# Query blocks turned through DRAM instead of TensorE, and six weight portions converted later, in an attention block followed by two MLPs

## The chip, the cores and the metric

One core of one Trainium2 chip. The metric is the device time of one execution, in microseconds (us): the median of the kernel before is 1572.41 us over three runs (1571.00 to 1572.81).

## The reference

Eight batches with eight heads of 576 positions and 64 features go through an efficient attention; its output is laid out as 4608 tokens of 512 features, which pass a first MLP with a hard gate and a second one with a sigmoid gate. All is float32.

```
q_s = softmax(q over features); k_s = softmax(k over positions)
x   = q_s @ (k_s.T @ v)              # per batch and head; then 4608 x 512
h   = x @ w_in;  g = h * clip(h + 3, 0, 6) / 6;  x = g @ w_out    # 512 -> 2048 -> 512
h   = x @ w2_in; g = h * sigmoid(h);             out = g @ w2_out
```

## The kernel before

Every product is made of matmuls on numbers split in two: a rounded upper part (fp32r) and the rest, three matmuls for one product (upper by upper, upper by lower, lower by upper). Twelve matmuls of 128x512 make one half step of an MLP.

**Blocks, units, stages.** The tokens are nine blocks of 512 (`NB`). The attention of a block is four units (`NP`), each a pair of heads, so there are 36 units, u = 0 to 35. The kernel has three stages:

- `first_block` does units 0 to 7 whole, a part of 8, the first MLP's weights and the first MLP on block 0.
- `middle` does the rest of the attention (q and x of units 8 to 35, k and v to unit 31) between the matmuls of the first MLP on blocks 1 to 4 (steps of `mm1`, L606, gate, `mm2`, L675). It also makes from both MLPs' weights the sums that the third stage needs, and stores them to DRAM (`ws`). Each of 16 portions of the second MLP's weights is loaded raw (`load_w`, L149), put together in float32 out of two words (`Conv`, L167: two scales on ScalarE, `shift`, `round`, `sign` on VectorE), split and stored (`Split`, L268), summed on GpSimd (`sums_in_place`, L244), split and stored again. The 16 portions of the first MLP's weights are already on the chip (`Resident`, L307).
- `second_mlp` runs six passes, each over a pair of blocks, with Strassen-like sums (seven products for eight), then the last block of the second MLP alone. `PASSES` (L112) orders them as (MLP, first block): (1,1), (0,5), (0,7), (1,3), (1,5), (1,7), 0 being the first MLP and 1 the second. A pass has 56 inner steps and 56 outer steps of six matmuls each; its weights come from `ws` through a ring of six buffers of 512 KB, each refilled as soon as it is used (`fetch`, L1268). Everything in a pass is put in order by a time in steps (`when`, L1254).

**The order in the middle** is written out: every piece of work is a job with an engine, and `MIDDLE` (L24) is the list of job numbers (two digits to base 64, the jobs numbered as `add` is called). Each engine runs its own jobs in that order; the keys (`begin`, `at`) do not decide there. SP issues all transfers, in order, so a transfer whose input is late holds back all that follow it.

**A unit's query path in the middle.** `q_max` (VectorE), `q_sub` (GpSimd, L491), `q_exp` (ScalarE), `q_sum`, `q_eps`, `q_recip`, `q_norm` (GpSimd, L520); then `q_turn` (L526), four TensorE transposes into PSUM, and `q_copy` (L553), ScalarE, into the tile `qt`; then `x_mm` (L561) multiplies `qt` by the unit's k-v product. There is one `qt` buffer (tag qT) and one `qe` buffer. The other way to turn it is in the code before but not used, since `DIRECT` (L1077) is above every unit: `q_blocks` (L535) transposes 32x32 blocks on VectorE, `q_store` (L543) writes 256 KB to DRAM and `q_load` (L546) reads it back in four DMAs of 64 KB with rows of 512 B, into the same `qt` buffer.

```
qt_ = add("PE", 0.65, key(3), lambda: q_turn(u), [qn], ["a", "qT"], ["qe"])    # L1118
ql = add("ACT", 0.62, key(3), lambda: q_copy(u), [qt_], [], ["a"])
...
ql = dma(1.4, key(4), lambda: q_load(u), 256, [z0], ["qT", "z"])               # L1123
```

**The first pass's operands** are seven sums and splits of its block pair, made at the end of the middle (`first_operands`, L1323, through `x_steps`, L1299); before they come from `yd`, where the first MLP has put blocks 1 and 2. The tiles `fixed` (L1394) collect a pass's eight results; they lie in the k and v buffers and in two tiles `fin`.

Of the kernel before, what the change touches and what calls it, by code (L numbers as in the profile page):

```python
# [18 lines left out]
P = 128  # L19
# [10 lines left out]
    "Lb1DBaBbC6LcC81nC9CACB1oDR1pLdLeLfLlCCLmCDLgLnCELQ0i1G1HLZLhLi0jA42M1I1-"  # L30
    "BcA51J0oLaLo0pLpLv1sLwLxLy1W1XCFBdLq1K1L1M1z0qLjBeA6CGCHCILrLs1SAL20Lk21222324C51bLzL-L_BRHLM3M425Lt"
    "Lu271T28M01YAM291_26E4M5M6M7MDCnE6AO2C2DMEM8MFANAPAQ2V1t1uM12NE7M2M9MAMGMNE8E9EAEB1vECEDFOFQFR2AARAS"
    "AdAeMBMHMIAT2B2k2W2XMJMC1eMK2EEEMOMPMQAf2jAgFSFTFUFVMXMYEFMLEGFWFXMZMaMR1f1gCl2FMMMS1h1i2t1jMTMUEkEm"
    "En2mMhMi2LMbMc2GAkMj2H2lFYFZMdMeMkMl2u2vMVMWDP1Z1a2I1k2wFaMm2x3a2J2KEoEpEqErEsEt2-"
    "MfMgAlAm1q2_3b30Mn2nMoG21r2o2pMpMqMvG4MtMx3j312q2rMz3ZMyEuEvEwM-AhM_N0N7N1MrMsG5G61wG72YG8G9N2N3N8N9"
    "2ZNA1xGAMuGBN4NBN52c392s2y1y2O2PNCND2d2eA_2zNHNINJ2QAi2f322R3k332S3l2TN6GCNENKNRNLGDAj38B0B23INMNSNT"
    "3B3J3K2UGE2aNUNVNF3A2bGhB1NG2gB3B4NWNNNO3L3MB5B62hB83C3-"
    "NX3cNP3_CmCoNY34Cp3D3E2i3F3GNbNcNdNe3P3Q3RCqCrB7NlB9BANfNgNmNnNoNQEjCsCt40BB3HCu3SBCBD3NNp3m3n3dNZNh"
    "NiCvBEBF48BHBoNqNaNjNv3O3T3qBIBJNrNs3rBpBqBK3e3f3g4PBrBsBt3hNwBLBGCwNxBOG13s3U3VNyNkNtNu49BPBQCxCyBM"
    "Bf3i3t3o4142NzN-N_O0O34A4R43O4O53pDQ4QO6444B45DSO7O8O9DT4COABuBv3uMw4S4647DUODOEOFOGO14nO2OBOCBgBN3v"  # L40
    "ONOHBwOI4D4F4GOODVDW4ZOJ4TBhBiBjBkDXDYOPOQ4HBlBm4U4VOK4IOROL4o4W4X4E4YOSHN3wCSDZ4J4a4b4K4xBxOXBy594e"
    "CT4c4dOYOTOUBzB-Bn4pOZ5ACVCUDaOMOa4f4gDbOhCW4yC2C34hDcOb4qC44iB_OiCXC0Oc4LOdC14r4zCJOjOkJKJMOVOW5J4s"
    "4tOfG34-"
    "Oe4j4kOlOmJNCYCZCa4_5CJOOnOo4u4vOrOsOtJPJQJROuOg4lO_CKJSOv4wCMCLCN50COCP5BJT515XOwOxCQP0P1P25D52OyOp"
    "OqP3P4P5I1CRP653HMHOCb5YJUJV4m5v5KHPP9PA5LJW545EPB5M5NFP5FHQHR5hPCPDPECcCdCe5QCiHSHT555wCjPJPKPLPMPN"
    "CfHUOz35POCk5R5S5T5657O-"
    "5GHV36Ig5ZIiPF5yIjCgChIkHWIlImP7374M3WP8PHPG5aHX5iInIo63PPPQ5HPIPR5jPS5k5l6465PVHYPbPcPdPTPe4N4OIp5I"
    "5O58PW3X3YCz5o5p5xPXPYPfPg5qPU5PPl5bIqIr5c66PmPnPo5d5ePZPa67PhPiPjC-"
    "D05fPpC_D1D25U5VPkD3IsPv6IPqPrPsD65g5m5nPwPxPyD45rPt6J6A6B5WD56R6SQ3Q4Q53xPzP-"
    "6CD7D96DQ66TP_D8DADBQ76U6VDCGiGk5s5t6gPuQ13yQ06HGlQ8Q9DDQADd3zQD6hQE5zQFQGGmGnGoGpGq6Y5-"  # L50
    "DeDEQNDgQ2QODFDGDH5_60GrQHDfDhDi615uDIDmQPQQ6268DJQIQR6pQJ69DjDK6q6K6L72DLQKDk6rQBQC6MQL6NDnDp71DlQS"
    "6OQTDoDqGsQXQYQZ6E6FDr7B6Z6fGtQaDs6P6Q6a6b6sQU6tEQGu6wDtQMQVDvDwQbQcQdQhQiER6iQe7C6WES6GQjQk7DQrQsQt"
    "DuDMDNDxETEU6jEVQl6k6lQmQW7Q6mEWEX6X6nQuQv6x6yEH6cDOQnQo6zExEIQfEY7RQw6o6uQ_EJDyE0E1EKELQgEME26v6-"
# [11 lines left out]
    "HtHuTVTPTQIITWTdTIUpIMH_9X8t8u9F9GHyHzTXTRTYH-IJ9YIKILTSTe9Z9aItTZTa9b9c9dUqINIPIOIQIRHvHwAp9e9H9IIS"
    "IT8xIVIWHxTfTgTnThTi8y8zIUToTpTq9fJ0Tj9JTbTcIXTk8-IuIv9gTlTrTsTxTyTzT-IwIxIyIz8_E5TtI-TuIY9091JXTmIZ"
    "IaU5U6U7U8J1J2J3J4I_T_UoUsTvJ59293J69KIbUmJgU0J7U1U2JYJZ9L9MIcJ89NIdU9TwUAJaJbUrUxUFUGJcUHUIBTUBUCU3"
    "U4JdJeJhUJJ9JAIeUDJB9O9PUuJiUKJzUvJCJDJEJjJkJlULUM9hJfUPUQURUSJmJnA7JFUT9Q9R9SJpJq9iUUUy94UZUaUbJGJo"
    "JH959TUc9U9VUdJIUEUNUOJrJsJtUVUeJuUXUWJvJwJxUfUgJyV1V2UtUYUwUzU-U_V0"
# [14 lines left out]
def efficient_attention_then_two_mlps(  # L84
# [1308 lines left out]
    def second_mlp(last):  # L1393
        fixed = []  # L1394
        for t in (kbuf[0], vbuf[0], kbuf[1], vbuf[1]):
            flat = t.rearrange("p a b c -> p (a b c)")
            fixed.append(flat[:, 0:BLK])
        for _ in range(2):
            t = raw.tile([P, 2, BLK], F32, tag="raw", name="fin")
            fixed += [t[:, 0], t[:, 1]]  # L1400
# [405 lines left out]
```

## Time and profile before

| | |
|---|---|
| median of three runs | 1572.41 us |
| profiled execution, its own time | 1573.07 us |
| its span, first to last instruction | 1571.4 us |
| TensorE busy | 1551.7 us (99%) |
| VectorE, ScalarE, GpSimd busy | 1187.0, 797.0, 548.7 us |
| moved by DMA | 358 MB, mean 228 GB/s |
| first block, to about | 140 us |
| middle, to about | 566 us |
| six passes, to about | 1480 us |
| last block of the second MLP | to 1571 us |

The span is what the trace covers; the time holds 1.7 us more around it. Matmuls are pipelined: in a stretch without a gap TensorE counts as busy whatever each matmul waits for, and what an instruction costs is read from the distance to the next start rather than from its own length.

### The profile page before, as it was taken

To read this page: it belongs to the slowest core of one execution; us is meant where nothing else is said; L and a number is where in the kernel's file an instruction comes from. 1 tells how busy PE (TensorE), PEld (TensorE's weight loads), DVE (VectorE), ACT (ScalarE), POOL (GpSimd) and SP (SyncE) were. 2 spreads that over 40 slices of the span, in tenths; PEclk is the share of its full clock that TensorE was granted. 3 is DMA by queue.
4 is the path that set the end of the run, shared out by engine and by line. 5 is a ranking of instruction groups with operands and counts; after the bars stand their busy time and mean duration, and the time that the engine had idled before them with its cause. 6 is when DMAs were issued, how large, how long until landed. Compare 5 with 4: busy or idle time off the path is not lost.

```text
span 1571.4 us, 22440 instructions
## 1 busy us (share of the span) xinstructions
PE 1551.7 (99%) x7415; PEld 1266.2 (81%) x7415; DVE 1187.0 (76%) x1849; ACT 797.0 (51%) x1433; POOL 548.7 (35%) x478
## 2 busy tenths in 40 slices
PE   7999999999999999999999999999999999999999
PEld 4787878878778788888888888888888888888887
DVE  7988777798888976895699459856986797677632
ACT  6886545556656643552365236533643464345422
POOL 4333664564454622222432242334223422440000
PEclk9999999999999999999999999999999999999999
DMA  9914767888889975667867656765768875889850
GB/s 270 344 44 143 243 221 242 259 279 273 262 249 323 289 272 195 220 218 209 229 227 248 218 192 220 259 208 197 239 202 214 223 248 192 228 229 368 259 131 27
DMA packets 342020, 358.02 MB, mean 228 GB/s; under 512 B 125200, under 2 KB 237072, under 8 KB 341904
## 3 DMA queue, kind: packets, MB, share of 16 engines
q1 hardware_dynamic: 340288, 355.90, 71.3%
q8 instruction: 59, 0.97, 0.3%
q10 hardware_dynamic: 1616, 0.69, 0.2%
q14 instruction: 57, 0.47, 0.1%
HBM read 269.48 MB, written 87.03 MB: 227 GB/s over the span
## 4 chain that ended last, share of the span: by engine, by line
PE 91%; DVE 4%; DMA 2%; ACT 1%; SPq 1%; issue 1%; POOL 0%; DVEq 0%; POOLq 0%; ACTq 0%
PE pb L1424 29%; PE pb L1583 29%; PE h L613 14%; PE y L688 12%; PE y L690 3%; PE pa L567 2%; PE pa L466 1%; PE pa L530 1%; DMA wo_early<-in_moe_w_out_dram 1%; DVE peaks L420 1%; DVE peaks L421 0%; DMA kbuf<-in_k_dram 0%; DVE fa L200 0%; DVE fa L196 0%; SPq L156 0%
## 5 line engine op out<-in xcount | busy, mean ns | idle before, releaser
L1424 PE MATMUL pb<-xo,ring 128*128 128x512 f32 x2016 | 459.1, 389 | 0.0
L1583 PE MATMUL pb<-gsp,ring 128*128 128x512 f32 x2016 | 458.9, 389 | 0.0
L1424 PEld LDWEIGHTS pb<-xo,ring 128*128 128x128 f32 x2016 | 378.4, 188 | 78.6
L1583 PEld LDWEIGHTS pb<-gsp,ring 128*128 128x128 f32 x2016 | 378.4, 188 | 78.6
L613 PE MATMUL h<-x,wi 128*128 128x512 f32 x1152 | 291.3, 397 | 2.1 <-POOL wi L221 0.9
L613 PEld LDWEIGHTS h<-x,wi 128*128 128x128 f32 x1152 | 213.1, 189 | 48.8 <-POOL wi L221 2.0
L1411 DVE TENSOR_TENSOR gsp<-g,gsp 128x512 fp32r<-128x512 f32 x288 | 222.9, 793 | 26.5 <-ACT gsp L1529 25.6
L688 PE MATMUL y<-g,wo 128*128 128x512 f32 x960 | 239.0, 396 | 0.0
L1529 ACT CAST gsp<-g 128x512 fp32r<-128x512 f32 x288 | 172.0, 621 | 123.8 <-PE pb L1583 108.2
L688 PEld LDWEIGHTS y<-g,wo 128*128 128x128 f32 x960 | 177.7, 188 | 38.9 <-issue 1.4
L1411 POOL TENSOR_TENSOR xst<-xst 128x512 f32<-128x512 f32 x40 | 90.1, 2253 | 207.9 <-DVE xo L1411 109.7
L1411 POOL TENSOR_TENSOR s<-U,s 128x512 f32<-128x512 f32 x40 | 53.2, 1331 | 217.7 <-DVE U L1411 217.7
L1411 POOL TENSOR_TENSOR g<-g 128x512 f32<-128x512 f32 x48 | 64.3, 1340 | 148.7 <-DVE g L1411 107.0
L1411 DVE TENSOR_TENSOR g<-r,pb 128x512 f32<-128x512 f32 x96 | 65.7, 685 | 54.5 <-ACT r L1438 54.1
L1438 ACT ACTIVATE r<-pb 128x512 f32<-128x512 f32 x96 | 57.1, 595 | 96.7 <-DVE pb L1411 72.5
L1411 DVE TENSOR_TENSOR U<-pb,s 128x512 f32<-128x512 f32 x96 | 66.1, 688 | 17.9 <-PE pb L1424 15.3
L626 ACT ACTIVATE r<-h 128x512 f32<-128x512 f32 x80 | 47.9, 599 | 59.4 <-PE h L613 54.7
L653 DVE SCALAR_TENSOR_TENSOR h<-r,h 128x512 f32<-128x512 f32 x80 | 55.0, 687 | 17.1 <-ACT r L626 17.0
L644 ACT CAST g<-h 128x512 fp32r<-128x512 f32 x80 | 46.9, 587 | 39.9 <-DVE h L653 28.5
L1411 POOL TENSOR_TENSOR spare<-g,g 128x512 f32<-128x512 f32 x48 | 64.0, 1334 | 3.8
L1438 ACT ACTIVATE r<-s 128x512 f32<-128x512 f32 x32 | 20.2, 633 | 87.6 <-POOL s L1411 70.6
L496 POOL TENSOR_TENSOR qe<-qraw,qm 128x512 f32<-128x512 f32 x34 | 38.0, 1117 | 76.4 <-PE pa L530 24.6
(159 smaller groups left out, 1921.0 us busy)
## 6 DMA issues: line engine op xcount, KB each, us to landing
ring<-ws SPq DMA_DIRECT2D x336, 512.0 KB, 3.8
ws<-sp SPq DMA_DIRECT2D x128, 256.0 KB, 3.5
wi_early<-in_moe_w_in_dram SPq DMA_DIRECT2D x16, 512.0 KB, 8.8
wo_early<-in_moe_w_out_dram SPq DMA_DIRECT2D x16, 512.0 KB, 9.7
...
ws<-w_sum SPq DMA_DIRECT2D x32, 256.0 KB, 2.9
ws<-fa SPq DMA_DIRECT2D x32, 256.0 KB, 3.0
...
```

What stands on the lines that cost most here:

```text
L496: eng.tensor_tensor(out=e.rearrange("p i h d -> p h i d"), in0=qt.pop(u), in1=live.pop(("qm", u)).to_broadcast([P, 2, NCH, D]), op=ALU.sub ...
L613: nc.tensor.matmul(h, w[:, a, c, :], x[:, e, c, :], start=(c == 0 and n == 0), stop=(c == NC - 1 and n == 2),)
L626: nc.scalar.activation(self.r, self.h, AF.Relu, bias=3.0)
L644: nc.scalar.copy(self.g[:, 0], self.r)
L653: nc.vector.scalar_tensor_tensor(out=self.h, in0=self.r, scalar=6.0, in1=self.h, op0=ALU.min, op1=ALU.mult)
L688: nc.tensor.matmul(y[c], w[:, a, cs], g[:, e, :], start=st, stop=sp)
L690: nc.tensor.matmul(y[c], g[:, e, cs], w[:, a, :], start=st, stop=sp, skip_group_check=c == NC - 1,)
L1411: (eng or nc.vector).tensor_tensor(out=out, in0=a, in1=b, op=how)
L1424: nc.tensor.matmul(to, ws_[:, a], e[:, c], start=p in ("P1", "P6", "P5") and c == 0 and m == 0, stop=c == 1 and m == 2, skip_group_check=True,
L1438: nc.scalar.activation(r, d[b, n, key], AF.Sigmoid)
L1529: nc.scalar.copy(t[0], source(p, i))
L1583: nc.tensor.matmul(d[b, p][m], w[:, a, m * P : (m + 1) * P], t[e], start=new and i == 0 and k == 0, stop=i == NPR - 1 and k == 2, skip_gro ...
```

## The change

- **The middle's queries.** `DIRECT` becomes 2*NP+1 = 9: of the middle's 28 units only unit 8 still uses `q_turn` and `q_copy`; units 9 to 35, 27 of them, go through `q_blocks`, `q_store`, `q_load`. `q_turn` no longer claims the `qt` buffer, `q_copy` does.
- **The passes.** `PASSES` becomes (0,5), (0,7), (1,1), (1,3), (1,5), (1,7). The first pass's operands are now built from attention outputs (`xq`) of blocks 5 and 6, so their four first loads wait for the stores of units 20 to 27.
- **Six portions.** The middle converts 10 of the 16 portions of the second MLP's weights. The other six (portions 2 to 7 of `w2_out`) are converted by `late_part` in the inner half of passes 0, 1 and 2, two in each, at steps 6 and 27 of the pass. They use `fin` for the raw words and `fixed`, the constants' tiles and the k-v tiles as buffers; the constants and the k-v tiles become slices of one tile each (`basis`, `kvs`), and `fixed` is dealt out anew so that both results from a `fin` tile are of one kind.
- **The order.** `MIDDLE` is a new list, of 1846 jobs instead of 1987. The order of `first_block` comes out the same as before.

```diff
-    PASSES = ((1, 1), (0, NCL), (0, NCL + 2)) + tuple((1, j) for j in range(3, NB, 2))
+    PASSES = ((0, NCL), (0, NCL + 2)) + tuple((1, j) for j in range(1, NB, 2))
...
-    kvt = [const.tile([P, P], F32, name=f"kv{i}") for i in range(KVS)]
+    basis = const.tile([P, 4 * P], F32, name="basis")
+    ident, peaks, halved = basis[:, 0:P], basis[:, P : 2 * P], basis[:, 2 * P :]
+    kvs = const.tile([P, 2 * BLK], F32, name="kvs")
+    kvt = [kvs[:, i * P : (i + 1) * P] for i in range(KVS)]
...
+    PARTS = 2 * NPR - 6
...
-        DIRECT = NB * NP
+        DIRECT = 2 * NP + 1
...
-                qt_ = add("PE", 0.65, key(3), lambda: q_turn(u), [qn], ["a", "qT"], ["qe"])
-                ql = add("ACT", 0.62, key(3), lambda: q_copy(u), [qt_], [], ["a"])
+                qt_ = add("PE", 0.65, key(3), lambda: q_turn(u), [qn], ["a"], ["qe"])
+                ql = add("ACT", 0.62, key(3), lambda: q_copy(u), [qt_], ["qT"], ["a"])
...
-            for n, c in enumerate(p.conv):
+            for n, c in enumerate(p.conv if k < PARTS else ()):
...
+            if at[0] == "b":
+                deps += [xstored[NCL + int(at[2]) - 1, 2 * int(at[1]) - 2 + n] for n in range(2)]
...
-        nc.sync.dma_start(to, yd[j, 2 * h : 2 * h + 2].rearrange("c p n -> p c n"))
+        nc.sync.dma_start(to, xq[j - FAR, 2 * h : 2 * h + 2].rearrange("c p n -> p c n"))
...
-            x_steps(1)["b12"]()
+            x_steps(NCL)["b12"]()
...
+        def late_part(i, t, a):
...
+            def scale(n):
+                nc.scalar.mul(a[n], words[n][:, :, 1].bitcast(F32), 2.0**-112)
+                nc.scalar.mul(words[n][:, :, 0], words[n][:, :, 0], 2.0**-29)
...
+            total = sums_in_place(1, a)
+            for fn, at in (
+                (load, (-5.0, -2.0)), (scale, (1.6, 5.6)), (shift, (2.6, 10.6)),
+                (round_up, (3.6, 11.75)), (sign, (4.75, 12.2)), (upper, (6.5, 12.9)), (upper, (20.2, 22.5)),
+            ):
+                for n in range(2):
+                    when(t + at[n], lambda n=n, fn=fn: fn(n))
+            for n in range(2):
+                when(t + (9.6, 16.6)[n], lambda n=n: lower(n, rest, nc.vector))
+                when(t + (10.8, 17.3)[n], lambda n=n: store(n, rest, NAMES[1][n]))
+                when(t + (21.6, 24.9)[n], lambda n=n: lower(n, a[n], nc.gpsimd))
+                when(
+                    t + (22.7, 26.3)[n],
+                    lambda n=n: store(n, a[n], [INTO[x] for x in NAMES[1][n]]),
+                )
+            for m in range(4):
+                when(t + 17.9 + 0.55 * m, total[m])
...
+        for n in range(2 * NPR - PARTS):
+            late_part(PARTS - NPR + n, 14 * NPR * (n // 2) + 6 + 21 * (n % 2), sums[n % 2])
```

## Rows read from the trace of the kernel before

**Rows 1.** The page's chain that ended last, by engine and by line.

```profile
PE 91%; DVE 4%; DMA 2%; ACT 1%; SPq 1%; issue 1%; POOL 0%; DVEq 0%; POOLq 0%; ACTq 0%
PE pb L1424 29%; PE pb L1583 29%; PE h L613 14%; PE y L688 12%; PE y L690 3%; PE pa L567 2%; PE pa L466 1%; PE pa L530 1%; DMA wo_early<-in_moe_w_out_dram 1%; DVE peaks L420 1%; DVE peaks L421 0%; DMA kbuf<-in_k_dram 0%; DVE fa L200 0%; DVE fa L196 0%; SPq L156 0%
```

**Rows 2.** Stretches: busy us by engine, granted clock, DMA share, GB/s.

```profile
160.00:566.00 406.00, 399.98 (x2191) 322.85 (x2190) 339.86 (x555) 235.91 (x437) 219.02 (x235) 1.00 0.83 263
566.00:642.00 76.00, 76.00 (x337) 62.94 (x336) 48.99 (x73) 30.18 (x51) 18.08 (x14) 1.00 0.66 224
718.00:795.00 77.00, 77.00 (x341) 63.79 (x340) 48.83 (x73) 27.29 (x49) 28.02 (x22) 1.00 0.83 223
```

**Rows 3.** TensorE's groups, 160 to 566 us: busy, mean ns, idle before, releaser.

```profile
L530 PE MATMUL pa<-ident,qe 128*128 128x128 f32 x106 | 16.0, 273 | 0.0
L426 PE MATMUL pa<-ident,peaks 128*128 128x128 f32 x21 | 6.2, 296 | 4.5 <-DVE ke L447 3.1 <-DVE peaks L421 1.2 <-ACT kv L483 0.2
L466 PE MATMUL pa<-vbuf,ke 128*64 128x65 f32 x440 | 17.7, 227 | 1.1 <-DMA xq<-xq 1.1
```

**Rows 4.** The chain of waits near 130 us: start, us, what.

```profile
129.68 0.73 PE pa L466 x20
130.41 0.59 PE pa L530 x4
...
136.22 2.72 PE y L688 x12
```

**Rows 5.** The same chain near 440 us.

```profile
441.58 0.44 PE pa L530 x4
```

**Rows 6.** TensorE in order of time near 330 and 468 us: start, us, [idle before].

```profile
329.71 0.66 PE L530 MATMUL pa<-ident,qe 128*128 128x128 f32 x4
...
468.07 0.47 PE L426 MATMUL pa<-ident,peaks 128*128 128x128 f32 x1 [2.46 <-DVE ke L447]
468.20 5.04 PE L613 MATMUL h<-x,wi 128*128 128x512 f32 x15
```

**Rows 7.** The clock in a stretch of 4 us after that gap, columns as in Rows 2.

```profile
468.00:472.00 4.00, 3.93 (x12) 3.19 (x13) 3.26 (x7) 1.55 (x3) 1.04 (x1) 0.61 0.98 354
```

**Rows 8.** DMA issues, 160 to 566 us: count, KB each, median us to landing.

```profile
ws<-sp SPq DMA_DIRECT2D x125, 256.0 KB, 3.5
xq<-xq SPq DMA_DIRECT2D x20, 256.0 KB, 3.2
qraw<-in_q_dram SPq DMA_DIRECT2D x4, 64.0 KB, 3.3
```

**Rows 9.** SP's queue near 342 us: start, us of issuing.

```profile
342.27 0.59 SPq L291 DMA_DIRECT2D ws<-sp  x1
346.22 1.29 SPq L366 DMA_DIRECT2D vbuf<-in_v_dram  x2
```

**Rows 10.** SP's waits, 160 to 566 us: total us, times, longest.

```profile
SPq L291 <- DVE fa L283: 17.8, 14, 3.5
...
SPq L291 <- POOL qe L522: 0.2, 1, 0.2
```

**Rows 11.** VectorE's conversion groups, 160 to 566 us, and a transpose from the page's groups.

```profile
L189 DVE TENSOR_SCALAR fa<-fa 128x512 uint32<-128x512 uint32 x30 | 18.2, 607 | 0.5 <-ACT fa L177 0.4
L196 DVE CUSTOM_DVE_ANT_0 fa<-fa,fr 128x1024 uint16<-128x1024 uint16 x30 | 25.5, 849 | 2.5 <-ACT kv L483 0.5 <-ACT fr L181 0.5
L200 DVE SCALAR_TENSOR_TENSOR fa<-wo_raw,fa 128x512 uint32<-128x512 uint32 x16 | 13.4, 836 | 0.4
L283 DVE TENSOR_TENSOR fa<-fa,sp 128x512 fp32r<-128x512 f32 x32 | 31.8, 995 | 1.8 <-ACT sp L280 1.5 <-POOL fa L251 0.2
L283 DVE TENSOR_TENSOR sp<-fa,sp 128x512 fp32r<-128x512 f32 x30 | 24.0, 799 | 4.3 <-ACT sp L280 3.7
...
L1631 DVE STREAM_TRANSPOSE gsp<-fin 128x512 f32<-128x512 f32 x12 | 8.5, 704 | 0.0
```

**Rows 12.** GpSimd's sums of a portion, all stages: busy, mean ns.

```profile
L251 POOL TENSOR_TENSOR fa<-fa 128x256 f32<-128x256 f32 x64 | 55.0, 859 | 24.8 <-DVE sp L283 19.6 <-DVE fa L200 1.4 <-POOL fa L251 0.7
```

More of the change, by code (lines that the diff above doesn't have):

```diff
@@ L30 @@
[L30 to L53, printed above, removed]
@@ L65 @@
[L65 to L69, printed above, removed]
+    "H-"
@@ new lines @@
+    "H_I000HMI6I8I9I4IAA8A90GIB0203010H090AAAABCYICI1IDIE04IFI2II0IDAIJIKIL0tIMAC0J0K0O0B0CAZAG05AbINISIT"
+    "IOIUI5IVIWAD0wAcAdAeAf0P0QI70D0XIPIX0E0V0eAIAgIGIHAH0F0L06IY0RBsIZIcAEAJ0uAKIdIeIf0YBDIgIhDq0fIQIRBE"
+    "HY0v0ZIa0a0b1G0MAh0c0d0jIi0xIjBFBG0yBH0gAiIm11AFAj0zI30WInHKGiIoIpIwIxFqIq0-"
+    "0_AkIr0h0i07IbIkIsAL10ItIyIzIlI-"
+    "1612130N0mIuIvJ4AMAN1JI_J0J1J21H1K0nBI08BJ1L1M1N1OJ5AO14151f1IAl1gJ6J7J8J9JAJE0SJFJGJ30kBKJBBL0o0pJH"
+    "JOJIJJJPJQJCJDAPAQ0T0UAR191AASAT1P22JKJRJL1i1V1j1QJY1RJZ1SHmJaJS1pJT1TBMJMJN1k1l1m1n1oJUJVJbJiJj170l"
@@ new lines @@
+    "1U25JW1B1YJcAVBt1Z1C1uJkJl1q2R23BvBwBuAWAXJdJeEWJfJsJt1rJm2C1s1t2627BNJuBxJn1xByJX1W1v28Bz292AJoJv0q"
+    "0r2qB-"
+    "0sAU1hJgJhJpJq18Jw2DJr1a1bBOBP2SK02UK1K2K32BB_1yJxJy2HJzKAH62V2W2X2YK4K5KB2Z3G242E2F2GK6K7C0KCKD2aAm"
+    "2K2g2tKEDC2u3i1D1z1-2b1EKF2v1F2w2x1X2yJ-J_K8Ho2L2MC12c2dKKKLC2C3H8KM2eKNKGKH2rK9AnAoKO2I2f3H2z33ApAq"
+    "ArKPCXCZ2TKIKQ1cAsKU2N3J34CaCbAvKVKR2JAtKWKJKXKYKZAuKmKaKSKT3KKnKbCc3L3M2j2-"
+    "KcKdKe2_1d1eKoKpKw30KxCdKqKr2hKsKi3Q482OCeCfKkKt2kHaKg2P2QKfKyKzK-"
+    "Ku312sK_3236L4KjL5L0Kv2lL1L6L71w1_CgAwAxAyAz3N3O3PA-Ds2mL23VL3ChL837KhA_20L9Ci21B0B2B3B4B5FA38LALBLE"
@@ new lines @@
+    "LF3j3R3SLGLHLO2i3s3t393u3l3T3UKl3W3mLI3nLJLKBQCj3oB1AaLPLC4B3I3pBR3q3rLLB94a3x2n2o4CB6B7LDBA35GgLMBT"
+    "LNLQLRLSLYLZ3YB8LaBSLbBB3yBUBVLT49LUDB3Z2p3ABZLWLcLdLe3a3bLVDDLX4DLfBW4z4E4F4A3B4d3v3w3-"
+    "3XLi4bBaBcDEDFLgLj4GBXLkLl4H4NLsLtLuLvBbLmBY3cLh3k4ILnLoBdBeLp4e4f4g4h4J4K4OC4BfBgM0M1M2M3Lq3d3zLwLx"
+    "Ly50Bh3_4k4lLzLrDGDHDI3e3C4mDJDK4i4j4LMAMBM440MCL-4M4-"
+    "C5M54p4QC74R41M6C6C8M74SC9BiBjBk42Bl5M4qMDMK51L_43Bp52MEBqDrDtDuMFDLDvDw4T4n4o4sMLMM53DM4cMNMOM85457"
+    "4P4_44DxMGM9MHDy584t5lMPDzDND-"
@@ new lines @@
+    "59MUMV554u5N5A5B5FMW5mMX565P5C4U5D5QMQMRCDMIMJ4V5oMSBrMe5R5S5TBmMYBnMZD_5U4v5WMTE05V5bMa5X5pMb5G5q5r"
+    "MfMg4r5HE1MhMoMpCEMi5cCA5Y5Z5sEVEXEYEZEaEb5vMjMkCG5a5tCBMlMqMrMsCFCH6XBoMcMd5u5I68MtMuMv4W6B5OEcEdCC"
+    "5wMyMz5-4wEU4xM-M_N6N7N85n5eCI5fN0N1MmMn696C6D6E6FEeN95x5y5gCJCK5E5zCL5_6wCM6GN26YN3CNMwMx6H6NCONANB"
+    "EfEg6aCPCQ6bNONPNQ6IF9FB4yNCNDN4Eh6OCTCU5JNR3D7J5hCRN5NENFFCNS5K6cNTNUNVNMFDFEFF61CVNYFG6dFH6e3E3FNZ"
+    "NaNbNcNI6f62CSNdNeCk5L6JNN6A6g6zFIClNGNf6KNiNjNkNKNlNsNtCn5dNHNLNJ6364CmCoNmNuCp6hCqCt6L6MNWNXFJFK6Z"
@@ new lines @@
+    "Nv6i6jFLNgNnNo6mNp6Q5i6-O0Fp5jO1O26RCrCuCvCwCxFrFsNwNx6xFtO3O46nNh6kNqNr6l60656_70NyCyN-Nz66FuFvOAO5"
+    "O67iOB5kGT6p6qOCOD6y71O7FwFxCs6S6TCzOK7K727MGV74756r6sOLOM73GW79C-"
+    "7T76D0N_6PONGXOEOFFyOOBC7778OPOGD1GYD2FzO8O97AOHD3C_OIOQF-OR6UGwGZGaGbD4D57U7V3f3g3h7N7O7P677Q7ROUOV"
+    "7S7YOWOXOYOe7C7LOJ6VOZOaOfOSOTF_GcGhD6Ob7DGdGe7EGj45GkGlGm7FGnOg7lOcOh466oOdGo47D7Gp7WOi6tOjOkD8Ol7X"
+    "7b7m6u85OoOpOqOr7j7nOyOz88GSOsO-"
+    "7o7p7q7rOtGfF8OuOvO_7cOmGqOnGrGs7Z7kDODP86Ow7s7t7B6W7xOx7dP0P1DR7eD9P2898AP6P7P87uDQDS7vP9GtDTDUGv6v"
@@ new lines @@
+    "En9WQeQS9X9YQfQgHHQh8THIQT8pQaQb949Z9aEBQoEoEpQi9jQjQk8q9b9cQpQqQlECEEHJEqEDSVQrQyEFEGQs8rQcQdEH9dEr"
+    "QtEIEKELGuEM8sEJQuEN9599QzQmQ-Q_QvEsEtR6R7EOEP9AEuEvFM9k9lSXR0EwExEyE-E_F09B989CEQR1QnQwQxEz9mR2R3F1"
+    "R8SYFNFOERESR9RARGRHRBF2F3RC9n9oRISaFPFQ9DFVFRRJR4F5ScF6R5REET9pF4RDRKRL9QHnFWFX9qHpHqRMRNRQF7FS9wFT"
+    "RRRSFYHrFZRTRUFaHsHtHuRVRFRaHvRWRX9r9EFU9RSbSfFbRbRc9x9y9zRdG0ReG1G3FcFeSdRO9eHwHxRfRPG29-"
+    "9FG4G5RkRlRm9fRgFdFfRnRoRYFgFhFiHyFoRh9s9_A0RZRiHzFjFkRu9gRvRwRjRxFlRpRqFmFnSeA19tShHLHNHOHPRrA2A3G9"
@@ L70 @@
+    "RyCWS2G6S3HQRzR-"
+    "G7S4S59hR_RsRtSCSDSiS6S7SESFG8HRHSGAHTGBGCGDS0S89uGESZGFS9SGGGSkGIGJGKSMSNSOA4GLA59SA6HUSHSlGMSPSQGH"
+    "SgGNSRS19vGPGQA79TGOSISjSJHVHWSASBGRSKSSSTSLHXSmSnSqSrSoSp"
 )
@@ L1082, in middle @@
         add = plan.add
-        n_k, n_q, n_v, qsub, ksub, kvmm, xmm, vlow, xready = ({} for _ in range(9))
+        n_k, n_q, n_v, qsub, ksub, kvmm, xmm, vlow, xready, xstored = ({} for _ in range(10))
         def dma(us, key, fn, kb, deps=(), take=(), give=()):
@@ L1144, in unit @@
             xs_ = dma(0.35, key(6), lambda: x_store(u), 256, [xc], [], ["t2k"])
+            xstored[j, pr] = xs_
             if j < NCL:
@@ L1178, in middle @@
                 done.append(parted(p.split[n], at + n + 0.2, [c3]))
-            for m, fn in enumerate(p.total):
+            for m, fn in enumerate(p.total if k < PARTS else ()):
                 done = [add("POOL", 0.68, at + 1.3, fn, done, [], [], True)]
-            for n in range(2):
+            for n in range(2 if k < PARTS else 0):
                 parted(p.split[2 + n], at + 1.4 + n, done, ["t2k"])
@@ L1337, in do @@
                 operand(name, 1)
-                x_steps(1)[name.lower()]()
+                x_steps(NCL)[name.lower()]()
             return do
@@ L1393, in second_mlp @@
     def second_mlp(last):
[L1394 to L1400, printed above, removed]
+        k0, v0, k1, v1 = (
+            t.rearrange("p a b c -> p (a b c)")[:, 0:BLK] for t in (kbuf[0], vbuf[0], kbuf[1], vbuf[1])
+        )
+        fin = [raw.tile([P, 2, BLK], F32, tag="raw", name="fin") for _ in range(2)]
+        fixed = [
+            x for m, (one, three) in enumerate(((k0, k1), (v0, v1)))
+            for x in (one, fin[0][:, m], three, fin[1][:, m])
+        ]
         whole = xs.tile([P, 4, 2, DM], F32R, tag="x", name="ring")
@@ L1618, in joins, with load, shift, round_up @@
                 when(t + k, lambda m=m, name=name: do(m, name))
+        words = [
+            t.rearrange("p a n -> p (a n)").bitcast(U32).rearrange("p (f t) -> p f t", t=2) for t in fin[::-1]
+        ]
+        sums = [(basis, kvs[:, 0:BLK]), (v0, k0)]
+        highs, rest = (kvs[:, BLK : 2 * BLK], v1), k1
+        def late_part(i, t, a):
+            def load(n):
+                nc.sync.dma_start(
+                    words[n].rearrange("p f t -> p (f t)"),
+                    w_src[1][1][(2 * i + n) * P : (2 * i + n + 1) * P, :].bitcast(U32),
+                )
+            def scale(n):
+                nc.scalar.mul(a[n], words[n][:, :, 1].bitcast(F32), 2.0**-112)
+                nc.scalar.mul(words[n][:, :, 0], words[n][:, :, 0], 2.0**-29)
+            def shift(n):
+                au = a[n].bitcast(U32)
+                nc.vector.tensor_scalar(
+                    out=au, in0=au, scalar1=3, scalar2=None, op0=ALU.logical_shift_left
+                )
+            def round_up(n):
+                au = a[n].bitcast(U32)
+                nc.vector.tensor_tensor(out=au, in0=au, in1=words[n][:, :, 0], op=ALU.add)
+            def sign(n):
+                au = a[n].bitcast(U32)
+                nc.vector.scalar_tensor_tensor(
+                    out=au, in0=words[n][:, :, 1], scalar=0x80000000, in1=au,
+                    op0=ALU.bitwise_and, op1=ALU.bitwise_or,
+                )
+            def upper(n):
+                nc.scalar.copy(highs[n].bitcast(F32R), a[n])
+            def lower(n, to, eng):
+                add(to.bitcast(F32R), a[n], highs[n], ALU.subtract, eng)
+            def store(n, lo, names):
+                part = Split(1, 1, i, None, names, None)
+                part.hi, part.lo = highs[n], lo
+                part.store()
+            total = sums_in_place(1, a)
[12 more added lines that the diff above has]
+                    lambda n=n: store(n, a[n], [INTO[x] for x in NAMES[1][n]]),
+                )
+            for m in range(4):
+                when(t + 17.9 + 0.55 * m, total[m])
```

30 lines of the change are left out of this document (8 added, 22 removed).

## The prediction

> **What bounds the kernel now.** Start with the chain that ended last: 91% of it is TensorE [rows 1]. Then cut the span into stages: in the passes TensorE is busy for all of each stretch of 76 us, and in the middle for 399.98 of 406 us [rows 2]. So the time is the sum of TensorE's instructions at their distance from start to start, plus a few gaps. In the middle these gaps are 6.0 us, nearly all before the k transposes, which wait for VectorE [rows 3]. One of 2.46 us let the granted clock fall: over the next 4 us it was 0.61, and 15 matmuls took 5.04 us [rows 6, 7], where twelve otherwise take 2.72 [rows 4], so 15 take 3.40: 1.6 us lost. VectorE, at 339.9 of 406 us, is second [rows 2]; SP is third. It issued 448 transfers there, from 0.59 to 0.65 us each [rows 9], and waited 169.4 us in 55 groups, whose first and last are shown [rows 10].
>
> **The change part by part.**
>
> **The transposes.** Removed: 27 units with four transposes each. On the chain a unit's four last 0.59 us [rows 4], 0.44 [rows 5] and 0.66 in order of time [rows 6]. I take 0.58, near the middle row: 27 x 0.58 = 15.7 us, all on TensorE, with bounds of 27 x 0.44 = 11.9 and 27 x 0.66 = 17.8. The same group's busy time, 16.0 us for 106 transposes, gives 16.3 for 108 [rows 3]. ScalarE's copies go too, but ScalarE is busy for 236 of 406 us and is not the bound [rows 2]: nothing.
>
> **The way through DRAM.** Added per unit: a VectorE transpose, 0.70 us [rows 11]; a store of 256 KB, 3.2 us to landing like the attention outputs' stores; four loads of 64 KB, 3.3 us like the smallest query loads [rows 8]; and five issues on SP. All of that can lie ahead of `x_mm` except one thing: there is a single `qt` buffer, so `q_load` of a unit cannot be issued before `x_mm` of the unit that TensorE did last. From there it takes (n + 4) issues at 0.62 us, n being the transfers listed between on SP, and 3.3 us to land. Queued behind a waiting `q_load` are SP's next stores and loads; behind a waiting `x_mm` is the whole of TensorE.
>
> Decoding the new list gives the TensorE work between two successive `x_mm`, summed at 2.72 us for twelve matmuls and 0.73 for a k-v product [rows 4], and n. For unit 13: six groups of three matmuls, a gate step's second product (1.81 and 0.91), a k-v product and a k transpose lie after `x_mm` of 14, 7.7 us; n = 7, so the load needs 11 x 0.62 + 3.3 = 10.1 us, 2.4 too long. In the same way: unit 15 has 9.9 against 11.4 (n = 9), 23 has 7.3 against 7.6 (n = 3), 25 has 12.9 against 14.5 (n = 14), 26 has 14.7 against 17.6 (n = 19). The other 22 fit, the nearest being 33 (6.8 against 6.4), 34 (8.8 against 8.3) and 32 (9.5 against 8.9). The shortfalls are 2.4 + 1.5 + 0.3 + 1.6 + 2.9 = 8.7 us. But some of the n transfers wait for nothing of TensorE and can be issued while it still works on the unit before; then nothing is short. From below the cost is 0. From above, each of the 27 comes late by as much as the mean wait that SP has today, 169.4 us in 191 waits, or 0.9 us [rows 10]: 24 us. I take 5, a little over half of 8.7, the only figure of the three that uses this order.
>
> SP's load: 27 x 5 = 135 transfers more; each portion moved out takes two loads and eight half stores away, 60 in all. 523 x 0.62 = 324 us of issuing, in a middle of some 395 us, against 448 x 0.62 = 278 of 406. There is room only if the waits shrink; here lies the risk.
>
> The Trainium skill speaks against this: VectorE: DVE Perf Modes, section Rules for kernel authors, says to transpose 128x128 on TensorE if PSUM may hold the result. It adds that VectorE's transpose makes only 32x32 blocks (section The three transpose paths). The trace has TensorE full, which that rule doesn't weigh; by the rule nothing would be won, and the time would be that of the second rival.
>
> **The six portions.** A portion costs VectorE in the middle 2 x (0.607 + 0.849 + 0.836) for putting together and 2 x (0.995 + 0.799) for the splits [rows 11], 8.2 us; six are 49 us. The 27 new transposes bring 19.0. So VectorE falls from 339.9 to about 310 us, 78% of 395 instead of 84%, and GpSimd by 6 x 4 x 0.86 = 20.6 us [rows 12]. What is late in the middle today is VectorE's k path; with less queued ahead of it I take back 2 of the 6.0 + 1.6 = 7.6 us of gaps and clock. Bounds: a gain of 7.6, and a loss of 2 if the denser order makes k later instead.
>
> In the passes the six cost nothing if TensorE stays covered. In an inner half VectorE is busy 49 of 76 us [rows 2]; two portions add at most 2 x 8.2, to 65. Each portion moves 3 MB, so two bring 83 GB/s in 76 us to the 222 to 224 there now, at a DMA share of 0.65 to 0.83; 0.83 stood there without a TensorE gap [rows 2]. The queues that the steps pass: ScalarE's second `upper` waits for GpSimd's four sums, 3.4 us [rows 12], 20.2 steps into a part; they are issued 2.3 steps before, 3.1 us at six matmuls, 1.36 us, a step. Behind it stand that half's copies and gates; a pair of gates is due only every seven steps, 9.5 us. SP's stores wait for VectorE with the weight fetches behind them, and these are issued twelve steps, 16 us, ahead. If that cover is gone, each portion costs TensorE about the 2.5 us of today's longest gap [rows 6] with its clock: up to 6 x 4 = 24. I take 0.
>
> **Pass order, operands, slices.** The passes do the same matmuls in another order: 0. The first pass needs units 20 to 27 stored; in the new list `x_mm` of 27 is more than 90 us of TensorE before the end. At the end of the middle three splits instead of two follow the last sum, some 2.5 us of ScalarE and VectorE, with about 12 us of TensorE work left: 0, at most 2.5. The constants become slices of one tile; if a slice waited for its neighbours, k's maxima would wait for TensorE. Both v buffers are slices of one tile now, and the k-v products wait for no load [rows 3]: 0, bound by 2.
>
> **The sum.** -15.7 + 5 - 2 = -12.7 us. The profiled execution took 1573.07 us (span 1571.4, 1.7 around it), so 1560.4; it lies 0.7 above the median of the runs. Against that median: 1560 us.
>
> **The rivals.**
>
> 1. *Also the waits go* (under 1554): the loads hide and the lighter VectorE gives back the gaps, -15.7 - 6 = -21.7, or 1551. For it: 22 of 27 units fit. Against it: an order is never free of gaps, and k's path is as long as before. 0.13.
> 2. *The waits eat the gain*: `q_load` lands late by about the 0.58 us that a unit wins, at every unit; -15.7 + 15.7 - 1, about 1571.5. For it: SP's 82% of issuing. 0.13.
> 3. *SP becomes the bound, slower*: transfers held back by late splits push every `q_load` behind `x_mm`. It decides where the mean delay exceeds 0.58 us plus the 2 us of relief shared by 27, 0.65 us. At 1.2 us it costs 27 x 1.2 - 15.7 = +17, about 1589, and some gaps of over 2 us add 1.6 each for the clock. For it: today's mean wait of SP is 0.9 us; against it: half of SP's waits today are those of a queue that is ahead, for TensorE hardly sees them [rows 3, 10]. 0.14.
> 4. *The passes open*: two portions per inner half delay gates or fetches, 6 x 2 = 12 us given back: 1572. Against it: an inner half has 27 us of VectorE free [rows 2]. 0.08.
>
> The forecast, between 1554 and 1567, has the other 0.52.
>
> **How the numbers follow.** 0.2%, about what a measurement can tell from no change, is 3.1 us. Faster takes the forecast, the first rival and a fifth of the second and fourth, 0.69; same takes most of these two, 0.14; slower takes the third and a little of them, 0.17. The range leaves out part of the first rival and the far half of the third: 1552 to 1580.
>
> **What would show it.** Right: 36 transposes instead of 144 on L530's successor, 9 units; middle shorter by 10 to 15 us; the passes still without a TensorE gap; TensorE's gaps in the middle under 15 us, the new ones before `x_mm`, with a DMA into `qt` as releaser, at units 13, 15, 25 and 26 first. Wrong: gaps before `x_mm` at most units, or of over 20 us in all (rivals 2 and 3); any idle time in passes 0 to 2 (rival 4); k's transposes later than today, which would take the 2 us back.

## The result and the profile after

| us | before | after |
|---|---|---|
| median of four runs each | 1572.61 (1571.00 to 1572.92) | 1553.34 (1553.17 to 1553.90) |
| profiled execution, its own time | 1573.07 | 1553.21 |
| first block, to its last piece before the middle | 136.06 | 135.66 |
| middle | 427.58 | 408.12 |
| six passes | 916.64 | 916.67 |
| last block, to the end of the span | 91.1 | 91.1 |

After to before is 0.988, 95% interval 0.9863 to 0.9897: 19.3 us faster. That lies in the range, on the side forecast, but 6.7 us below the predicted 1560, half as much gain again as forecast. At 1553.3 it is just inside the first rival's "under 1554".

The page's chain of the kernel after, by engine and by line, against [rows 1]:

```profile
PE 93%; DVE 2%; ACT 1%; DMA 1%; POOL 1%; issue 0%; SPq 0%; DVEq 0%; POOLq 0%; ACTq 0%
PE pb L1428 29%; PE pb L1587 29%; PE h L613 15%; PE y L688 12%; PE y L690 3%; PE pa L567 2%; PE pa L466 1%; DMA wi_early<-in_moe_w_in_dram 1%; DVE basis L420 0%; DMA ws<-sp 0%; PE pa L530 0%; POOL qe L496 0%; DMA qraw<-in_q_dram 0%; PE busy L933 0%; POOL wi L220 0%
```

TensorE's share grew: less of the chain is anything else. Next the stretches of the kernel after, the middle and then the inner halves of passes 0, 1 and 2, columns as in [rows 2]:

```profile
160.00:549.00 389.00, 387.14 (x2093) 311.73 (x2092) 309.76 (x523) 195.54 (x363) 200.89 (x209) 1.00 0.84 265
549.00:625.00 76.00, 76.00 (x337) 62.94 (x336) 62.41 (x91) 39.56 (x70) 31.05 (x26) 1.00 0.86 294
701.00:777.00 76.00, 76.00 (x337) 62.93 (x336) 57.53 (x81) 36.02 (x66) 41.34 (x34) 1.00 0.83 282
853.00:929.00 76.00, 76.00 (x337) 62.85 (x336) 56.93 (x80) 37.01 (x67) 41.31 (x34) 1.00 0.84 280
```

In the middle TensorE stands still for 1.86 us instead of 6.02. VectorE fell by 30 us, to the 310 that was forecast. In the passes VectorE went from 49 to between 57 and 62 us of 76, and GpSimd from 18 and 28 to as much as 41, and TensorE is still busy all the time. The waits of TensorE from 160 to 540 us, all there are (total us, times, longest):

```profile
PE pa L567 <- DVE x L586: 1.0, 1, 1.0
PE pa L426 <- DVE basis L421: 0.4, 1, 0.4
PE pa L438 <- DVE small L432: 0.2, 1, 0.2
PE h L613 <- DVE g L647: 0.2, 1, 0.2
```

No wait has a DMA into `qt` as releaser: the new wait, the largest risk of the prediction, costs TensorE nothing. TensorE's groups of 160 to 549 us, against [rows 3]; L530 has none left in this stretch:

```profile
L567 PE MATMUL pa<-qt,kvs 128*128 128x64 f32 (+4 forms) x140 | 30.1, 346 | 1.0 <-DVE x L586 1.0
L466 PE MATMUL pa<-vbuf,ke 128*64 128x65 f32 x440 | 17.7, 227 | 0.0
L426 PE MATMUL pa<-basis 128*128 128x128 f32 x21 | 6.0, 283 | 0.5 <-DVE basis L421 0.4
```

**What a group costs TensorE.** The mean lengths, 273 ns for L530 in [rows 3] and 283 for L426 here, overlap with the matmul after them. What counts is the distance from the start of one row to the start of the next. TensorE in order of time, in the kernel before; the first row follows the L530 row of [rows 6], the other two are the place of [rows 5]:

```profile
330.13 2.09 PE L613 MATMUL h<-x,wi 128*128 128x512 f32 x8
...
441.42 0.60 PE L530 MATMUL pa<-ident,qe 128*128 128x128 f32 x4
441.77 1.41 PE L688 MATMUL y<-g,wo 128*128 128x512 f32 x5
```

Four transposes that [rows 6] shows with 0.66 us began at 329.71, and the next matmul at 330.13: they hold TensorE for 0.42 us. The other four, 0.60 long, hold it for 0.35. Adding up these distances, less the idle time in brackets, over every row of the middle gives a sum that closes. Both middles run from the first L688 group after the first block to the first row of the passes: from 136.06 to 563.64 us before, from 135.66 to 543.78 after.

| us of TensorE in the middle | before | after | change |
|---|---|---|---|
| q transposes (28 groups; 1 group) | 11.31 | 0.36 | -10.95 |
| idle | 6.42 | 1.82 | -4.60 |
| `x_mm` | 24.25 | 22.72 | -1.53 |
| k transposes (46) | 3.75 | 2.36 | -1.39 |
| the MLP's matmuls | 364.27 | 363.18 | -1.09 |
| k-v products | 17.58 | 17.68 | +0.10 |
| sum | 427.58 | 408.12 | -19.46 |

**Where the new wait went.** TensorE around the units 14 and 13 (their `x_mm` are the L567 rows), and SP's queue in the same microseconds, kernel after:

```profile
243.30 1.21 PE L567 MATMUL pa<-qt,kvs 128*128 128x128 f32 x8
244.44 0.80 PE L466 MATMUL pa<-vbuf,ke 128*64 128x65 f32 x20
...
252.24 1.21 PE L567 MATMUL pa<-qt,kvs 128*128 128x128 f32 x8
```

```profile
244.04 0.63 SPq L370 DMA_DIRECT2D vbuf<-in_v_dram  x1
244.76 0.54 SPq L713 DMA_DIRECT2D yd<-o  x1
245.40 1.83 SPq L550 DMA_DIRECT2D qt<-zd  x4
247.34 0.38 SPq L291 DMA_DIRECT2D ws<-sp  x1
```

And the landing of the new transfers, 160 to 549 us, against [rows 8]:

```profile
qt<-zd SPq DMA_DIRECT2D x108, 64.0 KB, 2.8
zd<-qz SPq DMA_DIRECT2D x26, 256.0 KB, 3.1
```

`qt` is free at about 244.4. SP had by then only one transfer left in front of the loads; of the seven that the list puts there the others had gone. The loads go out from 245.40 to 247.23, 0.46 us each instead of 0.62 (over the 27 units the median is 0.49), and land 2.8 us later, by the median above, at about 250.0. `x_mm` of unit 13 begins at 252.24, so the margin of this unit is 2.2 us. The TensorE work between the two was put at 7.7 us and is 7.8; what was wrong is n: 7 where it was 1. SP issues 525 transfers in this stretch, summed over the DMA view's groups (523 forecast), and its waits fell to 96.7 us in 142, from 169.4 in 191 in the kernel before. The largest group of them shows SP ahead of TensorE: six times it stood in front of a `q_load` until `x_mm` had freed the buffer.

```profile
SPq L550 <- PE pa L567: 8.5, 6, 2.7
```

### The profile page after: what moved, and what is told of

It reads as the page before. It is cut to its first block, busy times and chain, and to the rows that moved or that the text cites. A ratio compares the mean times of both kernels' runs of the same rounds, so it can differ in the third digit from the quotient of the medians.

```text
span 1551.5 us, 22340 instructions
## 1 busy us (share of the span) xinstructions
PE 1537.7 (99%) x7307; PEld 1254.3 (81%) x7307; DVE 1193.8 (77%) x1864; ACT 781.3 (50%) x1406; POOL 569.3 (37%) x490
## 4 chain that ended last, share of the span: by engine, by line
PE 93%; DVE 2%; ACT 1%; DMA 1%; POOL 1%; issue 0%; SPq 0%; DVEq 0%; POOLq 0%; ACTq 0%
PE pb L1428 29%; PE pb L1587 29%; PE h L613 15%; PE y L688 12%; PE y L690 3%; PE pa L567 2%; PE pa L466 1%; DMA wi_early<-in_moe_w_in_dram 1%; DVE basis L420 0%; DMA ws<-sp 0%; PE pa L530 0%; POOL qe L496 0%; DMA qraw<-in_q_dram 0%; PE busy L933 0%; POOL wi L220 0%
## 5 line engine op out<-in xcount | busy, mean ns | idle before, releaser
L688 PE MATMUL y<-g,wo 128*128 128x512 f32 x960 | 236.8, 394 | 0.0
L688 PEld LDWEIGHTS y<-g,wo 128*128 128x128 f32 x960 | 178.0, 188 | 38.6 <-DVE g L647 0.2
L1442 ACT ACTIVATE r<-pb 128x512 f32<-128x512 f32 x96 | 56.9, 593 | 91.1 <-DVE pb L1415 69.6
L644 ACT CAST g<-h 128x512 fp32r<-128x512 f32 x80 | 46.8, 585 | 54.7 <-DVE h L653 43.1
L1415 POOL TENSOR_TENSOR spare<-g,g 128x512 f32<-128x512 f32 x48 | 69.2, 1442 | 3.8
```

What stands on the lines that cost most here:

```text
L644: nc.scalar.copy(self.g[:, 0], self.r)
L688: nc.tensor.matmul(y[c], w[:, a, cs], g[:, e, :], start=st, stop=sp)
L1415: (eng or nc.vector).tensor_tensor(out=out, in0=a, in1=b, op=how)
L1442: nc.scalar.activation(r, d[b, n, key], AF.Sigmoid)
```

## The experiments

Each kernel was timed beside the kernel before (1571.9 to 1573.1); intervals are ratios to it. It moved by up to 1.2 us between these sets of runs, so a difference between an experiment and the kernel after is good to about 1 us.

**1. The transposes put back into the kernel after.** They turn the loaded `qt` into the PSUM tile that `x_mm` then overwrites, so the product stays what it is; four more TensorE instructions per unit, nothing else.

```diff
+        for i in range(NCH if u > 2 * NP else 0):
+            nc.tensor.transpose(px[:, i * P : (i + 1) * P], qt[:, i * P : (i + 1) * P], ident)
```

> The changed kernel, with four TensorE transposes put back into x_mm of each of the 27 units that go through DRAM; they write into the tile that x_mm overwrites, so nothing but TensorE's time is added. Theory (the gain is TensorE work taken away, and the loads through DRAM hide): the time rises by 27 x 0.44 to 0.66 us, 12 to 18, from 1553.3 to 1565 to 1571. Rival (the new order did it, and the transposes had lain in gaps): it rises by less than 5.

Measured: 1563.87 us (0.9932 to 0.9959), 10.5 above the kernel after, 0.39 us a unit; less than the 12 to 18 that were expected. One such unit, TensorE in order of time:

```profile
245.40 0.60 PE L566 MATMUL pa<-basis,qt 128*128 128x128 f32 x4
245.83 1.21 PE L569 MATMUL pa<-qt,kvs 128*128 128x128 f32 x8
```

0.43 us from start to start; all 27 add up to 11.81 us. The other terms stay where the kernel after has them: 22.55 us for `x_mm`, 2.06 for the k transposes. So those two did not get shorter because the q transposes went.

**2. The same transposes elsewhere**, of a constant, into the step's own PSUM tile `h` ahead of 27 of the 64 steps of `mm1`: is 0.39 a matter of the place?

```diff
+        n = (j - 1) * NF + f
+        if ph == 0 and j and 0 in chunks and n * 27 // 64 != (n + 1) * 27 // 64:
+            for i in range(NCH):
+                nc.tensor.transpose(h[:, i * P : (i + 1) * P], ident, ident)
```

> The changed kernel with four TensorE transposes of the identity in front of 27 of the 64 first-MLP steps of the middle, into the tile that the step's matmuls overwrite: the same number as was taken away, and between long matmuls, as most of those stood. Theory (a group of four costs 0.44 to 0.66 us there, 0.58 in the mean): 14 to 18 us slower than the changed kernel, more than the 10.5 that four in front of x_mm cost. Rival (the price is 0.39 wherever they stand, and the rest of the gain is gaps): 10 to 12.

1564.06 us (0.9939 to 0.9964), 10.7 above, 0.40 a group: the rival came, not the theory. Within the 1 us, the price is the same in both places. In this trace the 27 groups hold TensorE for 9.62 us, 0.36 each, and the matmuls of `mm1` take 1.8 us more than in the kernel after.

**3. The pass order alone**, on the kernel before: new `PASSES`, operands from `xq`, one store of weight sums moved forward in the list.

```diff
-    PASSES = ((1, 1), (0, NCL), (0, NCL + 2)) + tuple((1, j) for j in range(3, NB, 2))
+    PASSES = ((0, NCL), (0, NCL + 2)) + tuple((1, j) for j in range(1, NB, 2))
```

> The kernel before with the new order of passes alone, its first operands from the attention outputs, and one store of weight sums moved forward in the middle since the first pass needs it. Theory: the passes hold the same matmuls, no change, within 1.5 us of 1572.6. Rival (part of the gain comes from the order of passes or the earlier operands): 3 us or more faster.

1575.17 us (1.0007 to 1.0025), 2.4 slower than before, more than the 1.5 of the theory. Two of TensorE's waits from 160 to 570 us:

```profile
PE pa L421 <- DVE ke L442: 3.1, 2, 2.5
PE pa L525 <- DVE ke L442: 1.6, 1, 1.6
```

The first is the kernel before's own [rows 3]. The second is new, a q transpose queued behind the same late k step, and would be 1.6 of the 2.4; the first pass starts 2.8 us later, 0.9 of it already in the first block. Its cause in the list was not followed further.

**4. The portions and the pass order, without the way through DRAM**: the list of before without the six portions' jobs, `DIRECT` as before.

```diff
+    PARTS = 2 * NPR - 6
...
-            for n, c in enumerate(p.conv):
+            for n, c in enumerate(p.conv if k < PARTS else ()):
```

> The kernel before with the new order of passes and the six portions converted in the passes, but all queries turned on TensorE as before; the middle's order is that of before without the portions' jobs. Theory (part of the gain is gaps that a lighter VectorE closes): 4 to 7 us faster than before, 1566 to 1569. Rival (all of the gain is the transposes): within 2 us of before.

1568.96 us (0.9969 to 0.9987): 3.8 faster than before, at the lower edge of the 4 to 7 expected, and 6.2 faster than the pass order alone. The middle:

```profile
160.00:559.00 399.00, 395.45 (x2177) 319.36 (x2176) 288.06 (x492) 207.78 (x388) 194.78 (x211) 1.00 0.71 224
```

VectorE has lost 52 us, and TensorE's gaps are 3.55 us instead of 6.02; the gap of 2.46 us is not there, nor the slow matmuls behind it. From here to the kernel after it is 15.6 us, the way through DRAM with its list. In TensorE's distances, 423.50 us of middle against 408.12: q transposes -10.95, idle -2.12, `x_mm` -1.35, k transposes -1.31, the rest +0.35; sum -15.38.

**5. The other half alone: the way through DRAM with all 16 portions still in the middle**, old pass order, the list of before edited by hand.

```diff
-        DIRECT = NB * NP
+        DIRECT = 2 * NP + 1
```

> The kernel before, with its order of passes and all 16 portions in the middle, but the 27 units' queries turned through DRAM. The order is that of before, edited by hand: q_blocks and q_store follow q_norm, q_load follows x_mm of the unit before, x_mm and what follows it stand up to 9 us later. Theory (VectorE with 19 us more and SP with 135 transfers more have no room while the portions are there): gaps take the 15.6 back, 1568 to 1595. Rival (the parts simply add up): 1556 to 1560.

1650.16 us (1.0492 to 1.0521), 78 slower than before, far beyond both expectations. TensorE's longest waits, and then SP's from 160 to 640 us:

```profile
PE h L609 <- DVE g L643: 16.9, 12, 4.6
PE pa L422 <- DVE peaks L417: 10.3, 5, 6.0
```

```profile
SPq L540 <- DVE qz L534: 34.1, 14, 5.9
SPq L546 <- DMA zd<-qz: 29.2, 14, 4.4
```

SP stands in front of 14 loads until the store just ahead of them has landed: the edited list put them too close together. How much of the 78 us is this list's is not shown; the run doesn't price the way through DRAM at a full VectorE with a list made for it.

**6. All 16 portions back in the middle of the kernel after**, the list merged by hand, TensorE's order that of the kernel after.

```diff
-    PARTS = 2 * NPR - 6
+    PARTS = 2 * NPR
```

> The changed kernel with all 16 portions of the second MLP's weights converted in the middle again, none in the passes; TensorE's order is that of the changed kernel, the portions' jobs stand where the order before had them, merged by hand. Theory (a lighter VectorE and SP close the gaps and let the loads hide): 3 to 10 us above the changed kernel, 1556 to 1563, with gaps before k's transposes and before x_mm. Rival 1 (the portions' place is worth nothing): 1553 to 1555. Rival 2 (SP becomes the bound): above 1568.

1747.93 us (1.1101 to 1.1131), 195 above the kernel after, where 3 to 10 were expected. TensorE's longest waits:

```profile
PE h L610 <- DVE g L644: 65.4, 15, 10.6
PE y L685 <- ACT g L641: 30.1, 6, 11.3
```

Gates stand for 10 us behind conversions that the merge put right after their loads: in this trace ScalarE's first step of a conversion waits 58.7 us in all for raw weights, and VectorE's next step 61.3 us for ScalarE. The run is inconclusive on what the portions' place is worth; with the last one it suggests that each list fits one set of jobs.

**7 and 8. More transfers for the same bytes**: `q_load` in 8 pieces of 32 KB, and in 16 of 16 KB.

```diff
-            nc.sync.dma_start(t[b * 32 : b * 32 + 32].rearrange("x (a n) -> x a n", a=4), zb[b])
+            for s in range(0, 32, 16):
+                nc.sync.dma_start(
+                    t[b * 32 + s : b * 32 + s + 16].rearrange("x (a n) -> x a n", a=4),
+                    zb[b, s : s + 16],
+                )
```

> The changed kernel with each q_load in 8 DMAs of 32 KB instead of 4 of 64 KB: some 1.7 us more of SP's issuing at 0.43 us each between one x_mm and the next, 46 us in all. Theory (SP is ahead, so a load goes out as soon as the buffer is free; margins from landing to x_mm of about 2 us at units 13, 23 and 33 and more elsewhere): 0 to 2 us slower. Rival (the prediction's shortfalls: the transfers in front are issued only after x_mm of the unit before): 8 to 15 us slower.

> The same with 16 DMAs of 16 KB: 5.2 us more per unit, 139 us in all, more than the 97 us that SP still waits in the middle. Theory: the six or seven units with margins under 5 us open by 1 to 3 us each, and SP falls behind at others: 10 to 30 us slower than the changed kernel. Rival (SP's margin is wide): under 5.

1580.23 us (1.0030 to 1.0055), 27 above the kernel after, and 1633.18 (1.0370 to 1.0401), 80 above: both far beyond what was expected. The longest wait of TensorE and one load on SP with 8 pieces, then the same with 16:

```profile
PE pa L571 <- DMA qt<-zd: 8.0, 3, 3.9
```

```profile
310.00 3.83 SPq L551 DMA_DIRECT2D qt<-zd  x8
```

```profile
PE pa L571 <- DMA qt<-zd: 35.4, 12, 5.8
```

```profile
278.94 6.89 SPq L551 DMA_DIRECT2D qt<-zd  x16
```

A load takes twice as long to issue with 8 pieces, and a margin of 2.2 us is gone. From 300 to 325 us SP issues with hardly a pause, so what is queued behind comes late as well. SP's waits in the middle fall from 96.7 us in the kernel after to 66.8 with 8 pieces and 62.2 with 16. This looks like the third rival's mechanism, transfers held back behind SP, with 108 issues more; the 8 us at `qt` are not the whole of the 27.

**9. Issues off the load's own path**: four transfers of 512 B behind each `q_load`, which nothing waits for.

```diff
+        for b in range(4):
+            nc.sync.dma_start(junk[u, b, 0:1], ident[0:1])
```

> The changed kernel with four DMAs of 512 B issued behind each q_load: SP's issuing grows by some 40 us, as with the loads in 8, but the way of a load to x_mm doesn't. Theory (SP's queue as a whole is near its limit): 10 to 27 us slower. Rival (the loads in 8 cost what they did since each load itself came later): 0 to 5.

1567.00 us (0.9958 to 0.9982), 13.7 above, or 0.13 for each tiny transfer. The middle, and one such group on SP:

```profile
160.00:557.00 397.00, 385.55 (x2072) 308.52 (x2071) 304.37 (x519) 195.75 (x362) 198.76 (x209) 1.00 0.81 256
```

```profile
248.40 1.82 SPq L551 DMA_DIRECT2D qt<-zd  x4
250.26 1.16 SPq L553 DMA_DIRECT2D junk<-basis  x4
```

TensorE's gaps are 11.45 us, ten waits of at most 2.2 us, and only 0.7 us of them are for a load into `qt`. That points to the whole of SP's queue having little room, not only the loads; the run doesn't separate SP's issuing from the load on the DMA engines behind it.

**10 and 11. VectorE**: the block transpose of each unit done twice (19 us more in the middle), and three times (38 us).

```diff
+        for _ in range(2):
             nc.vector.transpose(
```

> The changed kernel with each block transpose on VectorE done twice instead of three times: 19 us more of VectorE. Theory (VectorE is just short of its limit, each us over it costs): 2 to 8 us slower, less than half of the 21.5 that 38 us cost. Rival (in proportion): 10 to 11.

> The changed kernel with each of the 27 block transposes on VectorE done three times: 38 us more of VectorE in the middle, some 348 of 389, nothing else changed. Theory (VectorE's load made the gaps before): 2 to 6 us slower. Rival (the gaps depended on the order alone): within 1 us of the changed kernel.

1561.15 us (0.9920 to 0.9945), 7.8 above, at the upper end of the 2 to 8 expected; and 1574.86 (1.0006 to 1.0024), 21.5 above, a miss. With three, the middle and TensorE's first two waits:

```profile
160.00:565.00 405.00, 386.90 (x2071) 308.05 (x2070) 342.73 (x574) 194.88 (x362) 204.72 (x211) 1.00 0.80 251
```

```profile
PE h L614 <- DVE g L648: 7.3, 6, 2.3
PE pa L426 <- DVE basis L421: 4.9, 5, 1.2
```

VectorE is then busy for 343 of 405 us, as long as in the kernel before [rows 2]; the gates and k come late, and the whole gain is gone. A microsecond more of VectorE costs 0.41 us with two and 0.57 with three (0.45 and 0.55 when each set's own runs of the kernel before are the measure).

## Why the prediction was right, and where its sum was off

**Transposes, -15.7 forecast, 10.5 to 10.9 measured.** The mechanism held, the price did not: 0.58 us a unit was the length of a piece of the chain [rows 4] and of a row up to its modelled end [rows 6]. From start to start a unit holds TensorE for 0.40 (11.31 / 28), below even the lower bound of 0.44. Experiments 1 and 2 say the same in device time, 0.39 and 0.40.

**The new wait, +5 forecast, 0 measured.** This step failed outright, at its lower bound. It counted every transfer between a load and the unit before as still to be issued at 0.62 us; SP was ahead, an issue of a load took 0.49 in the median, and the five units named short are not. But the margin of unit 13 is 2.2 us, and experiments 7 to 9 show how soon the cost comes.

**Gaps and clock, -2 forecast, about -6 measured.** Idle time fell by 4.60 us, and the MLP's matmuls by 1.09, near the 1.6 put down to the clock. The list of the kernel after goes further than experiment 4, where TensorE is idle for 2.1 us more. This is the first rival's mechanism ("also the waits go"), which was given 0.13: k hardly waits any more (0.6 us), and VectorE is 30 us lighter. Of the 6.0 us of gaps before, 4.5 stood in front of k transposes and 1.1 in front of a k-v product [rows 3]; that one is gone too.

**Not in the sum at all: -2.9** in `x_mm` and the k transposes. They hold TensorE for less time although they do the same. Experiment 1 rules out that the transposes' leaving did it; experiment 4, with the old list, doesn't have it. What differs is what stands behind them in TensorE's order. Over the middle before, a k transpose holds TensorE for 0.04 us in the mean when an MLP matmul follows and for 0.15 otherwise; after, for 0.04 and 0.17. In the list before 29 of the 46 have an MLP matmul behind them, in the new list 42. So at 141.51 us before, a k transpose is followed by a k-v product 0.20 us later; at 240.43 after, by an MLP matmul 0.03 later.

```profile
141.51 0.27 PE L426 MATMUL pa<-ident,peaks 128*128 128x128 f32 x1
141.71 0.80 PE L466 MATMUL pa<-vbuf,ke 128*64 128x65 f32 x20
```

```profile
240.43 0.27 PE L426 MATMUL pa<-basis 128*128 128x128 f32 x1
240.46 3.00 PE L613 MATMUL h<-x,wi 128*128 128x512 f32 x12
```

With `x_mm` it is the same: 17 of 28 have an MLP matmul behind them before, 25 after. Four matmuls of 128x128 hold TensorE for 0.97 us in front of a k-v product, in the kernel before, and for 0.58 in front of an MLP matmul, in the kernel after:

```profile
152.82 1.03 PE L567 MATMUL pa<-qt,kv 128*128 128x128 f32 x4
153.79 0.80 PE L466 MATMUL pa<-vbuf,ke 128*64 128x65 f32 x20
```

```profile
151.84 1.03 PE L567 MATMUL pa<-qt,kvs 128*128 128x128 f32 x4
152.42 3.20 PE L613 MATMUL h<-x,wi 128*128 128x512 f32 x12
```

As an estimate, the new neighbours at the prices of the kernel before give -1.3 us for k and -1.2 for `x_mm`, of the -1.39 and -1.53 measured. So most of this part is the new list's order; no run changes the neighbours alone, and for the ScalarE copies that went no more than the other 0.4 us would be left.

**The portions in the passes, 0 forecast, 0 measured** (916.64 and 916.67 us), so the fourth rival fell. **Pass order, 0 with at most 2.5:** alone it costs 2.4, but the whole change doesn't show it. As steps the medians are +2.4 (pass order), -6.2 (portions) and -15.6 (the way through DRAM with its list), together -19.4. Each of these steps also has a list of its own.

**The sum.** Forecast -15.7 + 5 - 2 = -12.7. Measured in the trace -10.95 - 4.60 - 1.09 - 1.53 - 1.39 + 0.10 = -19.46 in the middle, and -0.40 in the first block, whose length lies between 135.3 and 137.0 us in the traces of the experiments. Two errors of 5 us, in the transposes and in the wait, cancelled, and that is luck; what was left over is the gaps and the neighbours. The time came out in the first rival's place, which had 0.13, and 1.3 us above the lower end of the range, while the forecast's own stretch of 1554 to 1567 had 0.52. The second and third rival did not come, but they were not far: with 108 issues or 38 us of VectorE more, the gain is smaller or gone. The six portions made room on both: they took 49 us of VectorE and 60 transfers out of the middle. In experiment 4 that is worth 6.2 us by itself; that the way through DRAM could not have paid without it is argued from experiments 7 to 11 and not shown, since experiments 5 and 6 had lists that did not fit.

The Trainium skill's advice to transpose 128x128 on TensorE where PSUM may hold the result (VectorE: DVE Perf Modes, Rules for kernel authors) did not hold here: with TensorE full, taking 27 units from it and giving them to VectorE and the DMA queue won most of the 15.6 us.
